# Storing the second half of the last nine output tiles from ScalarE's queue

## The chip, the core and the metric

The kernel runs on one core of a Trainium2 chip. The core has five engines with instruction streams of their own: TensorE (PE in the profile), VectorE (DVE), ScalarE (ACT), GpSimd (POOL) and SyncE (SP). They meet only at semaphores. SyncE computes nothing; here it issues DMAs. Sixteen DMA engines move the data of all queues. The metric is the device time of one execution in microseconds (us); lower is better.

## What is computed

```python
scores = scale * np.matmul(q_c, k_c.transpose(0, 1, 2, 4, 3))   # chunks of 64 positions
attn = softmax(scores)
x = (attn @ v_c), heads side by side                            # [8, 576, 512]
theta = x @ w_theta
zr, zi = x * np.cos(theta), x * np.sin(theta)
y = einsum('ts,bsd->btd', w_tok_r, zr) + einsum('ts,bsd->btd', w_tok_i, zi)
u = x + y
out = u + np.maximum(u @ w_ch, 0.0)                             # [8, 576, 512] float32
```

The inputs `q`, `k`, `v` have the shape 8 x 8 x 576 x 64 in float32. The first three lines are attention within chunks of 64 positions; the rest mixes positions (`w_tok_r`, `w_tok_i`) and channels (`w_theta`, `w_ch`).

## The kernel before

The eight batches are worked in four pairs, `p` = 0 to 3 (`NP` is 4). A pair has 1152 positions, cut into nine tiles of 128 rows, numbered `j` = 0 to 8. Tile 4 (`MID`) is shared by both batches; every other tile belongs to one batch and holds two blocks of 64 positions that lie 128 positions apart in the output. So a result tile has two row halves, `half[0]` (partitions 0 to 63) and `half[1]` (64 to 127), and each half goes to another place of the output.

The order of all work is written out by hand in the list `ORDER`. A step such as `W.35.0` names the work, the pair, the tile and, where needed, a buffer slot; the instructions of each engine follow this list. The last part of the list works on pair 3 and holds, for each tile, these steps:

- `Y` (line 482): 9 accumulating matmuls of 512 columns (18 of half the rows for tile 4) give y on TensorE.
- `y` (line 490): VectorE adds x and writes the tile `u`.
- `Ud` (line 507): SyncE issues a DMA transpose of `u` into `uT`. For the last tile, 30, TensorE transposes instead (`U`, line 499), and VectorE copies (`uv`, line 513).
- `W` (line 519): 4 matmuls with `w_ch`.
- `w` (line 528): VectorE computes max(., 0) + u and writes the float32 tile `o32`, of which there are four buffers.
- `st` (line 543): two DMAs, one for each row half, store the tile.
- `D` (line 156): a matmul on a blank tile, whose result nothing uses.

SyncE's queue holds, in the order of the list, the stores of line 543 and the DMA transposes of lines 400 and 507. The list ends as follows (the last line holds the end of the program):

```text
Ud.35 W.35.0 Ud.37 st.38 W.36.1 w.35 st.35 w.36 st.36 W.37.0 U.30.1 uv.30 w.37 W.30.1
D.00.0 D.00.0 D.00.0 D.00.0 st.37 w.30 st.30 D.00.1 D.00.0 D.00.1 D.00.0 D.00.1 D.00.0
```

Each DMA has a completion semaphore, one of a small set that is used in turn. At the end of the program SyncE waits for all landings, and then the engines meet at a barrier (both appear under line 623). ScalarE issues no DMA in this kernel: it computes exponentials, sines and cosines, and some copies. Its last compute instruction is the sine of step `g.3D`, which stands in the list ahead of the first store of pair 3 (`st.32`).

Of the kernel before, what the change touches and what calls it, by code (L numbers as in the profile page):

```python
# [68 lines left out]
def kernel(  # L69
# [11 lines left out]
    nc = tc.nc  # L81
# [6 lines left out]
    NP = B // 2  # L88
# [18 lines left out]
    half = [slice(0, CH), slice(CH, P)]  # L107
# [425 lines left out]
    def store(p, j):  # L533
        o = st[p].pop(("o", j))
        if j == MID:
            to = [out[2 * p + b, KT * P : S, :] for b in range(2)]
        else:
            bb = int(j > MID)
            jl = j - bb * (MID + 1)
            s0 = (jl // 2) * GT + (jl % 2) * CH  # L540
            to = [out[2 * p + bb, s0 + r * P : s0 + r * P + CH, :] for r in range(2)]
        for r in range(2):
            nc.sync.dma_start(to[r], o[half[r]])  # L543

# [42 lines left out]
        "W": w,  # L589
        "w": relu_add,  # L590
        "st": store,
    }
    with tc.manual_schedule():
# [34 lines left out]
```

## Time and profile before

| What | us |
|---|---|
| median of 6 runs | 212.7 |
| lowest and highest of them | 211.34, 214.14 |
| the profiled execution | 213.83 |
| its span, first to last instruction | 212.1 |
| TensorE busy in it | 194.5 |
| VectorE busy | 134.4 |
| ScalarE busy | 89.1 |
| GpSimd busy | 105.4 |

The profiled execution is one run of its own; 1.7 us of its time lie outside the span. The engine names end in q where an instruction is the sequencer's own: it waits, or issues a DMA, and the engine is not counted as busy. A DMA's row gives when its issue begins and how long the queue is held; when the data have landed is told apart, as the time from the beginning of the issue. The 72 stores of line 543 have 128.0 KB each (64 rows of 2 KB), and land 2.5 us after their issue began, in the median.

### The profile page before, as it was taken

The numbers are of one execution on the slowest core, as the hardware profiler recorded it, in microseconds if no ns is written. First come the engines' busy times: TensorE is split into PE (matmuls) and PEld (weight loads), VectorE is DVE, ScalarE is ACT, GpSimd is POOL, SyncE is SP. The second block draws the span as 40 slices with busy tenths as digits, with TensorE's granted clock in tenths as the row PEclk, the third lists the DMA queues.
The fourth block names the chain that finished last, engine by engine and source line by source line (L and its number), as shares of the span: only waits on it lengthen the run. The fifth ranks groups of instructions, "written<-read, shape, count | busy, mean of one in ns | idle before, by whom it ended". The sixth has DMA issues, their size and how long they took to land.

```text
span 212.1 us, 6378 instructions
## 1 busy us (share of the span) xinstructions
PE 194.5 (92%) x2790; PEld 96.8 (46%) x2790; DVE 134.4 (63%) x243; ACT 89.1 (42%) x91; POOL 105.4 (50%) x131
## 2 busy tenths in 40 slices
PE   7838879999999999999999999949969999999983
PEld 2414435655555654455554555414434443444431
DVE  1402856978878948987773997545864762845360
ACT  2004477455923477857319929643002563000000
POOL 8799989988998999789799000000000000000000
PEclk9995899999999999999999999987999999999999
DMA  6999999999999999999999920684668677845756
GB/s 199 273 154 146 151 173 160 166 165 163 169 202 151 139 169 180 200 188 200 152 156 201 148 49 2 151 106 96 143 96 168 128 149 150 179 96 121 152 117 144
DMA packets 137947, 32.09 MB, mean 151 GB/s; under 512 B 130624, under 2 KB 132288, under 8 KB 137920
## 3 DMA queue, kind: packets, MB, share of 16 engines
q0 software_dynamic: 113744, 15.43, 114.0%
q1 hardware_dynamic: 24176, 16.26, 33.8%
q8 instruction: 22, 0.36, 0.7%
q14 instruction: 5, 0.04, 0.1%
HBM read 33.06 MB, written 9.44 MB: 200 GB/s over the span
## 4 chain that ended last, share of the span: by engine, by line
PE 67%; DMA 15%; POOL 8%; DVE 4%; issue 3%; SPq 2%; ACT 0%; POOLq 0%
PE ps_y L482 27%; PE ps_theta L413 12%; PE ps_uw L519 12%; DMA qk<-in_k_dram 7%; POOL qk L173 5%; PE ps_idle L156 4%; PE ps_qkT L269 4%; DMA qk<-in_q_dram 3%; DMA xT<-x 3%; POOL v L181 3%; PE ps_sT L315 3%; PE ps_x L348 3%; DMA uT<-u 2%; SPq L543 1%; PE ps_uT L499 1%
## 5 line engine op out<-in xcount | busy, mean ns | idle before, releaser
L482 PEld LDWEIGHTS <-wT 128*128 128x128 f16 (+1 forms) x360 | 30.8, 100 | 35.2 <-issue 1.6
L482 PE MATMUL ps_y<-zr,wT 128*128 128x512 f16 (+1 forms) x180 | 45.0, 380 | 0.2 <-ACT uT L513 0.2
L482 PE MATMUL ps_y<-zi,wT 128*128 128x512 f16 (+1 forms) x180 | 42.0, 379 | 0.0
L490 DVE TENSOR_TENSOR u<-ps_y,x 128x512 f16<-128x512 f32 x36 | 24.7, 689 | 27.2 <-PE ps_y L482 27.2
L519 PE MATMUL ps_uw<-wch,uT 128*128 128x512 f16 x144 | 36.8, 386 | 3.5 <-DMA uT<-u 3.0
L173 POOL DMA_DIRECT2D qk<-in_q_dram x40 | 34.6, 898 | 5.4 <-PE ps_qkT L269 1.4
L413 PE MATMUL ps_theta<-wtheta,xT 128*128 128x512 f16 x144 | 34.6, 385 | 2.1 <-DMA xT<-x 2.1
L173 POOL DMA_DIRECT2D qk<-in_k_dram x40 | 34.6, 892 | 3.8 <-DMA qk<-in_q_dram 1.8
L181 POOL DMA_DIRECT2D v<-in_v_dram x40 | 34.4, 896 | 1.2 <-DMA v<-in_v_dram 0.5
L429 ACT ACTIVATE cos<-ps_theta,pihalf 128x1024 f16<-128x1024 f32 (+1 forms) x20 | 20.6, 1029 | 34.3 <-PE ps_theta L413 33.4
L328 ACT ACTIVATE eT<-ps_sT 128x1024 f16<-128x1024 f32 (+1 forms) x20 | 18.6, 938 | 35.2 <-PE ps_sT L315 35.1
L528 DVE SCALAR_TENSOR_TENSOR o<-ps_uw,u 128x512 f32<-128x512 f32 x36 | 24.7, 688 | 11.9 <-PE ps_uw L519 11.3
L361 DVE TENSOR_TENSOR x<-ps_x,recip 128x512 f16<-128x512 f32 (+1 forms) x40 | 25.5, 638 | 1.4
L413 PEld LDWEIGHTS <-xT 128*128 128x128 f16 x144 | 13.8, 100 | 19.9 <-DMA xT<-x 3.1
L519 PEld LDWEIGHTS <-uT 128*128 128x128 f16 x144 | 13.0, 98 | 18.5 <-DMA uT<-u 3.3
L156 PE MATMUL ps_idle<-blank 128*128 128x512 f16 x60 | 19.8, 459 | 1.4 <-DVE pihalf L144 1.2
L433 ACT ACTIVATE sin<-ps_theta 128x1024 f16<-128x1024 f32 (+1 forms) x20 | 18.7, 934 | 0.0
L294 DVE COPY qkT<-ps_qkT 128x2048 f16<-128x2048 f16 x12 | 14.6, 1220 | 5.6 <-PE ps_qkT L269 5.6
L269 PE MATMUL ps_qkT<-id,qk 64*128 64x64 f16 x576 | 12.4, 193 | 3.6 <-DMA qk<-in_k_dram 3.5
L269 PEld LDWEIGHTS <-qk 64*128 64x128 f16 x576 | 10.1, 96 | 7.9 <-DMA qk<-in_k_dram 3.9
L360 DVE RECIPROCAL recip<-ps_x 128x8 f32<-128x8 f32 (+1 forms) x40 | 7.8, 196 | 7.3 <-PE ps_x L348 7.1
L442 DVE TENSOR_TENSOR zr<-x,cos 128x1024 f16<-128x1024 f16 x16 | 10.9, 684 | 1.0 <-ACT cos L429 1.0
(43 smaller groups left out, 138.2 us busy)
## 6 DMA issues: line engine op xcount, KB each, us to landing
out_dram<-o SPq DMA_DIRECT2D x72, 128.0 KB, 2.5
qk<-in_q_dram POOLq DMA_DIRECT2D x32, 128.0 KB, 7.0
qk<-in_k_dram POOLq DMA_DIRECT2D x32, 128.0 KB, 6.4
v<-in_v_dram POOLq DMA_DIRECT2D x32, 128.0 KB, 6.1
theta<-in_moe_w_theta_dram SPq DMA_DIRECT2D x1, 1024.0 KB, 8.4
tok<-in_moe_w_tok_i_dram SPq DMA_DIRECT2D x1, 576.0 KB, 4.1
tok<-in_moe_w_tok_r_dram SPq DMA_DIRECT2D x1, 576.0 KB, 5.3
qk<-in_q_dram POOLq DMA_DIRECT2D x8, 64.0 KB, 8.6
```

The source lines that it names most:

```text
L156: nc.tensor.matmul(ps, blank[:, 0:P], blank, start=True, stop=True)
L173: nc.gpsimd.dma_start(nats[p, g][rows, which, r], (q, k)[which][b, :, t0 : t0 + n, :].rearrange("h s d -> s h d"),)
L181: nc.gpsimd.dma_start(v16[rows, slot + r, :, 0:D], v[b, :, t0 : t0 + n, :].rearrange("h s d -> s h d"),)
L269: nc.tensor.transpose(psv[:, r, w, e, j, :], t[half[r], w, j, 2 * e : 2 * e + 2, :].rearrange("s h d -> s (h d)"), id16[half[r], half[r]],)
L361: nc.vector.tensor_tensor(out=st[p]["x"][:, j0 : j0 + n, f * NE * D : (f + 1) * NE * D].rearrange("p c (h d) -> p c h d", h=NE), in0=psv[: ...
L413: nc.tensor.matmul(ps[:, j * DM : j * DM + DM], xT[:, j * NDB + db, :], wtheta16[:, db, :], start=(db == 0), stop=(db == NDB - 1),)
L429: nc.scalar.activation(out=cos[:, 0:n].rearrange("p a e -> p (a e)"), in_=pin, func=AF.Sin, bias=pihalf, scale=1.0,)
L433: nc.scalar.activation(out=sin[:, 0:n].rearrange("p a e -> p (a e)"), in_=pin, func=AF.Sin)
L482: nc.tensor.matmul(ps[rows], wT[:, kt, cols], z[:, jz, :], start=(kt == 0), stop=(kt == 2 * KT),)
L490: nc.vector.tensor_tensor(out=u, in0=st[p].pop(("ps_y", j))[:, 0:DM], in1=st[p]["x"][:, j], op=ALU.add)
L519: nc.tensor.matmul(ps, uT[:, db * P : db * P + P], wch16[:, db, :], start=(db == 0), stop=(db == NDB - 1),)
L528: nc.vector.scalar_tensor_tensor(out=o, in0=st[p].pop(("ps_uw", j)), scalar=0.0, in1=u, op0=ALU.max, op1=ALU.add)
```

## The change

In pair 3 (`p == NP - 1`), the store of the second row half (`r == 1`) of each of the nine tiles is issued from ScalarE's queue; the store of the first half stays in SyncE's. Nine of the 72 stores move. The addresses, the sizes and the list `ORDER` stay as they are.

```diff
         for r in range(2):
-            nc.sync.dma_start(to[r], o[half[r]])
+            queue = nc.scalar if p == NP - 1 and r else nc.sync
+            queue.dma_start(to[r], o[half[r]])
```

## The prediction

> **What bounds the kernel now.** I read the chain of work that ended last first, because only what lies on it is worth time, and then its last stretch in order of time. By engine, the chain is this:
>
> ```profile
> PE 67%; DMA 15%; POOL 8%; DVE 4%; issue 3%; SPq 2%; ACT 0%; POOLq 0%
> ```
>
> Most of it is TensorE. The stores of pair 3 begin at 189.3 us, so only the end matters. The table of waits says whether TensorE waits for anything there (window 176.5 to 206 us; columns: who, for whom, us in total, times, longest):
>
> ```profile
> PE ps_uw L519 <- DVE uT L513: 0.5, 1, 0.5
> PE ps_theta L413 <- DMA xT<-x: 0.4, 1, 0.4
> ```
>
> The second wait is over before the first store of pair 3, and the first is the VectorE copy of tile 30. From 180 to 200 us TensorE is busy 5.00 of every 5.00 us. So no store and no transpose on SyncE holds TensorE, and a freer SyncE cannot make the matmuls earlier. What is left is the tail behind the last matmul. Three views show it: VectorE's timeline, SyncE's timeline, and the line of the final waits (start, duration, engine, line, what; in the last two rows min/median/max in ns, then first and last start).
>
> ```profile
> 204.98 0.68 DVE L528 SCALAR_TENSOR_TENSOR o<-ps_uw,u 128x512 f32<-128x512 f32 x1
> 206.20 0.69 DVE L528 SCALAR_TENSOR_TENSOR o<-ps_uw,u 128x512 f32<-128x512 f32 x1 [0.53 <-PE ps_uw L519]
> ```
>
> ```profile
> 203.25 0.47 SPq L543 DMA_DIRECT2D out_dram<-o  x1
> 203.77 1.59 SPq L543 DMA_DIRECT2D out_dram<-o  x1
> 205.46 0.55 SPq L543 DMA_DIRECT2D out_dram<-o  x1
> 206.74 2.47 SPq L543 DMA_DIRECT2D out_dram<-o  x4
> 208.62 0.59 SPq L543 DMA_DIRECT2D out_dram<-o  x1
> ```
>
> ```profile
> L623 SPq EVENT_SEMAPHORE  x12: 17/28/28, 209.3 to 212.0; - x12
> L623 PEldq DRAIN  x2: 13/222/430, 208.6 to 211.6; - x2
> ```
>
> The last result tile (30) is ready at 206.20 + 0.69 = 206.89. SyncE begins its two stores only at 208.03 and 208.62: it is 1.14 us late, because it still has the stores of 36 (ready 204.17, issued from 205.46) and 37 (ready 204.98 + 0.68 = 205.66, issued 206.74 and 207.34) in hand. Neighbouring stores start about 0.64 us apart, so a tile costs SyncE 1.28 us, and tiles 35, 36, 37 and 30 come 0.94, 1.49 and 1.23 us apart. On top, one issue took 1.59 us instead of 0.59. The trace's packets show a 16 KB instruction packet from 203.76 to 204.99; five other stores that began in such a packet (at 110.84, 120.12, 132.90, 153.34 and 177.97) took 1.05 to 1.72 us and ended some 0.4 us after it, as this one did.
>
> The last store lands at about 208.62 + 2.35 = 210.97 (its own landing is not recorded; second halves beside it land after 2.3 to 2.4 us, and SyncE's wait ends at 211.0). From there to the end of the span at 212.06 are 1.09 us of last waits and barrier.
>
> **The change, part by part.**
>
> *Removed from SyncE:* nine issues of 0.59 us, 5.3 us in all. Ahead of 201 us this only makes the transposes of 35 and 37 start earlier; TensorE does not wait for them, so the worth is nothing. If that cover were gone (a transpose landing later than its matmuls are due), the least margin is that of tile 35: landing 198.53 + 2.4 = 200.9, used at 201.5, 0.5 us. The change takes issues out from ahead of it, so the margin grows.
>
> *Added to ScalarE:* nine issues. ScalarE's last compute instruction starts at 179.47 and takes 1.02 us; the first moved store is ready after 189 us. Each new store waits for VectorE's result, and behind that wait stand only later stores and the final barrier. Nobody else waits for ScalarE. Its cost is nothing until the last tile.
>
> *Semaphores:* completion semaphores are reused every eighth DMA, and each issue waits for the one before on its semaphore. The closest case is the very last store: its predecessor on the semaphore was issued at 201.77 and landed at about 204.1, 2.8 us before 206.9. No stall. A second set of semaphores would give SyncE up to eight more final waits of some 0.06 us (their spacing); those ahead of the last landing are hidden, so 0 to 0.3 us, taken as nothing.
>
> *The tail, with both queues issuing at once.* Tile 35: both halves at 203.25; SyncE's takes 0.47, so both can be through before the packet at 203.76. Tile 36: ready at 204.17, inside the packet, both held to about 205.37. Tile 37: ready at 205.66, both begin at 205.69 and end by 206.28. Tile 30: ready at 206.89, both queues are free and begin at 206.92 (SyncE follows VectorE by 0.03 us at 203.25). The 1.1 us of lateness is gone, and the second half no longer stands behind the first.
>
> Landing of tile 30: a store whose queue was waiting for it lands 2.24 us after its start (that of 192.74), so the first at 209.16. The second half's data move beside it. At the 273 GB/s of the page's busiest slice 128 KB need 0.48 us, so both have landed by 209.16 + 0.48 = 209.64. If the halves overlap wholly, it is 209.16. I take 209.6, because the two share the DMA engines. Gain: 210.97 - 209.6 = 1.4 us; bounds 1.3 and 1.8. TensorE's last blank matmul and its drain end at 208.6 + 0.43 = 209.0, so they don't take over as the end.
>
> *ScalarE's issue time* is the unknown: the trace has no DMA issued there. From below, SyncE's own 0.47 us; from above, the longest ordinary issue of another kind, 1.24 us for a DMA transpose. With 1.24 us its stores of 35 to 30 begin at 203.25, about 204.5 (held to 205.8 at most), 205.8 and 207.0, and the last lands some 0.7 us after a short one: gain 0.7. I take SyncE's value, as the instruction is the same, and keep 0.7 for the range.
>
> *Two rules that speak against the change.* The row: SyncE's 0.59 us is held per store, whatever it moves, since the 1 MB load of w_theta took less:
>
> ```profile
> 1.75 0.47 SPq L212 DMA_DIRECT2D theta<-in_moe_w_theta_dram  x1
> ```
>
> The Trainium skill, "DMA: Bandwidth & Descriptors", section "Rules for kernel authors", says of two transfers to disjoint partition halves: "Don't bother — they serialize", and that several issuing engines only save issue time. By that rule the data gain nothing (I have let them serialize: 0.48 us), and all that counts is issue time. Here issue time is what is late, so the sum stays 1.4. The sharper rule is in "Perfetto Trace Analysis", section "DMA Instruction — HWDGE (DVE, Sync)": one descriptor generator is shared by the two issuing sequencers and locked while one uses it. If the lock covers the whole 0.59 us, ScalarE's second half of 35 runs into the instruction packet as now, and the six stores behind it follow one another from 205.37: 36 to 206.55, 37 to 207.73, and 30 begins its halves at 207.73 and 208.32 instead of 208.03 and 208.62. That is a gain of 0.3 us. Against it stands the row above: eight times the rows of a store (512 of 2 KB against 64) in no more time, so that making descriptors is a small part of an issue and the lock short. I go by the row: 1.4, not 0.3. No run here shows two issuing queues of this kind side by side.
>
> **The sum.** 213.83 - 1.4 = 212.4 us for the profiled execution, span 212.1 - 1.4 = 210.7. That execution lies 1.1 us above the median of the runs; the tail behind the last matmul does not depend on what made it longer, so the median goes from 212.7 to 211.3, 0.65% less.
>
> **The rivals.**
>
> *A, the shared generator serializes the issues.* Gain 0.3 us (0.1 to 0.7), median 212.4. For it: the rule. Against it: the 0.47 us for 1 MB.
>
> *B, slower: ScalarE issues slowly.* Place: its last four stores, from 203.25. They follow one another, so at T each the last begins at 203.25 + 3T. This passes today's 208.62 from T = 1.8 us on, three times SyncE's cost. At T = 2.4 the last begins at 210.45, 1.8 us later than now: 214.5. For it: GpSimd's issues take 0.89 us, so issues are not alike on all engines. Against it: no undisturbed issue in the trace takes over 1.24 us.
>
> *C, the forecast's gain with another beside it, over 1%.* The tail alone can give at most 206.92 + 2.24 = 209.16 against 210.97, 1.8 us or 0.85%. Over 1% would need something ahead of the tail, where I find no wait: 210.2. That the change does not do what it says (the moved stores not the last ones) is excluded by the list: `st.30` is the last store, and its second half moves.
>
> **How the numbers follow.** Forecast 0.66, A 0.18, B 0.08, C 0.08. Within 1% (about what a measurement of this kernel can tell from no change) are the forecast and A: 0.84. The forecast's own range is 210.9 to 212.0. The range reaches over A to 212.9, and down to 209.9, since the six runs of before already spread from 211.34 to 214.14; B's upper part and the lower part of C stay out.
>
> **What would show it.** Right: SyncE's last store begins at about 206.9 us and ScalarE's within 0.1 us of it, with issues of about 0.6 us; the last landing comes at about 209.6; TensorE's busy time and its last matmul stay. Wrong: ScalarE's issues of 1.1 us or more, beginning with SyncE's (the lock, A); ScalarE's stores running late behind one another (B); TensorE's matmuls with `w_ch` waiting for `uT`; or the end set by something other than the last landing.

## The result, and the profile after

The changed kernel took 211.64 us (median of 29 runs, 209.57 to 215.93) against 212.72 us (66 runs, 209.35 to 216.23) for the kernel before. The ratio is taken over the runs that lie within 1.5% of the fastest run of the same kernel, 31 of the 66 and 19 of the 29. It is 0.9974, with a 95% interval from 0.995 to 0.9999: a gain of 0.55 us, between 0.02 and 1.06. The forecast was 1.4 us. So the direction held, and the gain stayed within 1% as forecast, but its size was missed.

In the profile after, the execution took 210.01 us and its span 208.2 us. The page shows the second queue (queue, kind, packets, MB, share of 16 engines), and its chain of work that ended last, by engine:

```profile
q1 hardware_dynamic: 23456, 15.08, 30.6%
q10 hardware_dynamic: 720, 1.18, 2.2%
...
PE 80%; DMA 8%; DVE 4%; POOL 3%; issue 2%; SPq 2%; ACT 1%; ACTq 0%; POOLq 0%
```

TensorE carries the chain as before. Its table of waits in the last stage (174 to 203.5 us) is word for word that of before, so nothing was won or lost there:

```profile
PE ps_uw L519 <- DVE uT L513: 0.5, 1, 0.5
PE ps_theta L413 <- DMA xT<-x: 0.4, 1, 0.4
```

The tail, in the timelines of VectorE, SyncE and ScalarE (start, us, engine, line, what), for the last two results and the last two tiles' stores:

```profile
202.43 0.68 DVE L528 SCALAR_TENSOR_TENSOR o<-ps_uw,u 128x512 f32<-128x512 f32 x1
203.65 0.69 DVE L528 SCALAR_TENSOR_TENSOR o<-ps_uw,u 128x512 f32<-128x512 f32 x1 [0.54 <-PE ps_uw L519]
```

```profile
201.65 0.88 SPq L544 DMA_DIRECT2D out_dram<-o  x1
203.14 0.47 SPq L544 DMA_DIRECT2D out_dram<-o  x1
204.37 0.47 SPq L544 DMA_DIRECT2D out_dram<-o  x1
```

```profile
201.65 0.85 ACTq L544 DMA_DIRECT2D out_dram<-o  x1
203.15 0.50 ACTq L544 DMA_DIRECT2D out_dram<-o  x1
204.38 0.50 ACTq L544 DMA_DIRECT2D out_dram<-o  x1
```

The last result is ready at 203.65 + 0.69 = 204.34, and both queues begin its stores at once, 0.03 us later. Each issue is short, though the two run side by side. The line of the last pair of stores gives their landings (min/median/max of the two), and the line of the final waits gives the end:

```profile
DMA to landing us min/median/max: 2.4/2.5/2.7
```

```profile
L624 SPq EVENT_SEMAPHORE  x12: 17/28/28, 204.9 to 208.2; - x12
```

The halves land 2.39 and 2.70 us after their issue, the second at 207.08. That is 2.74 us after the last result; in before it was 210.97 - 206.89 = 4.08, by the prediction's estimate of the last landing.

Since executions differ ahead of the tail, I cut each span at two points: the first theta matmul of group 3D, which stands ahead of every instruction that the change touches, and the end of the last `w`.

| us | to the cut | middle | tail | span |
|---|---|---|---|---|
| before | 176.53 | 30.36 | 5.17 | 212.1 |
| after | 173.98 | 30.36 | 3.88 | 208.2 |

The middle, in which the nine moved stores are issued, is equal to 0.01 us. The tail is 1.29 us shorter. The other 2.55 us of the two spans' difference lie ahead of the change and are none of its doing. Outside the span the two executions need 1.77 and 1.79 us, so the change costs nothing there either.

### The profile page after: what moved, and what is told of

Same layout as the page of the kernel before. It is cut to its first block, busy times and chain, and to the rows that moved or that the text cites. A ratio compares the mean times of both kernels' runs of the same rounds, so it can differ in the third digit from the quotient of the medians.

```text
span 208.2 us, 6386 instructions
## 1 busy us (share of the span) xinstructions
PE 192.9 (93%) x2790; PEld 96.4 (46%) x2790; DVE 134.4 (65%) x243; ACT 89.1 (43%) x91; POOL 105.2 (51%) x131
## 4 chain that ended last, share of the span: by engine, by line
PE 80%; DMA 8%; DVE 4%; POOL 3%; issue 2%; SPq 2%; ACT 1%; ACTq 0%; POOLq 0%
PE ps_y L482 31%; PE ps_theta L413 15%; PE ps_uw L519 14%; PE ps_qkT L269 5%; PE ps_idle L156 4%; DMA qk<-in_k_dram 4%; PE ps_x L348 3%; PE ps_sT L315 3%; POOL qk L173 3%; DMA xT<-x 3%; DMA uT<-u 2%; PE ps_uT L499 2%; PE ps_xT L379 2%; DVE x L361 1%; SPq L544 1%
## 5 line engine op out<-in xcount | busy, mean ns | idle before, releaser
L519 PE MATMUL ps_uw<-wch,uT 128*128 128x512 f16 x144 | 35.9, 380 | 2.9 <-DMA uT<-u 2.4
L413 PE MATMUL ps_theta<-wtheta,xT 128*128 128x512 f16 x144 | 33.9, 379 | 1.1 <-DMA xT<-x 1.1
```

The source lines that it names most:

```text
L413: nc.tensor.matmul(ps[:, j * DM : j * DM + DM], xT[:, j * NDB + db, :], wtheta16[:, db, :], start=(db == 0), stop=(db == NDB - 1),)
L519: nc.tensor.matmul(ps, uT[:, db * P : db * P + P], wch16[:, db, :], start=(db == 0), stop=(db == NDB - 1),)
```

## The experiments

The theories: **1**, the tail gains 1.0 to 1.35 us in every execution, and the comparison of full kernels is too coarse for it; **2**, the tail gains so much, but the second queue costs 0.6 to 0.8 us elsewhere; **3**, the tail of before hangs on a 16 KB instruction packet, so its first profile showed more lateness than there always is.

**Both kernels again (e1, e2).** No edit but a comment.

> The kernel before, once more, against itself. All theories: ratio 1.000. Looked at: the stretch from the end of the last w (line 528) to the end of the span, 5.17 us in the profile of before. Theory 1 (the tail gains 1.3 us in every execution and nothing else changes; the comparison is too coarse for it) and theory 2 (the tail gains 1.3 us, and something ahead of it costs 0.8 us) say 5.1 to 5.2 us again. Theory 3 (the length of the tail of before hangs on where the 16 KB instruction packet falls, and the profiled execution had a long one) says a shorter tail, 4.2 to 4.9 us.

> The changed kernel once more. Theory 1: tail 3.85 us, the stretch from the first theta matmul of group 3D to the end of the last w 30.4 us as in both profiles, ratio 0.9935 (0.991 to 0.996). Theory 2: that stretch, or the one before it, is 0.8 us longer than in before, ratio 0.997. Theory 3: tail 3.85 us and ratio 0.996 to 0.998, because the tail of before is usually shorter than in its first profile.

Measured: e1 against before 0.9976 (0.9911 to 1.0042), so a kernel against itself is known to no better than 0.65%. e2: 0.9989 (0.993 to 1.0047). These ratios decide nothing. The cuts do: e1 has a middle of 30.37 and a tail of 4.91, e2 has 30.46 and 3.82. SyncE's timeline in e1 shows the issue that meets the packet, and the last two stores; VectorE's row is the last result:

```profile
200.72 1.32 SPq L543 DMA_DIRECT2D out_dram<-o  x1
...
204.70 0.55 SPq L543 DMA_DIRECT2D out_dram<-o  x1
205.29 0.59 SPq L543 DMA_DIRECT2D out_dram<-o  x1
```

```profile
203.15 0.69 DVE L528 SCALAR_TENSOR_TENSOR o<-ps_uw,u 128x512 f32<-128x512 f32 x1 [0.54 <-PE ps_uw L519]
```

Here the packet took 1.02 us and not 1.23, the issue was held 1.32 us and not 1.59, and SyncE was 204.70 - 203.84 = 0.86 us late, not 1.14. So the lateness moves with the packet, and the gain is 1.09 us between these two. No middle is 0.8 us longer, which speaks against theory 2.

**Without the packet in the tail (e3, e4).** The first 24 `D` steps are taken out of `ORDER` in before (e3) and in the changed kernel (e4), so that the packet, which comes after a fixed number of TensorE instructions, falls behind the end.

```diff
-ones.00 D.00.0 D.00.1 lw.01 cw.01 lw.00 D.00.0 q.0M D.00.1 D.00.0 D.00.1 D.00.0 D.00.1
-D.00.0 D.00.1 D.00.0 q.0B q.0A cw.00 k.0M D.00.1 D.00.0 D.00.1 D.00.0 D.00.1 D.00.0
+ones.00   lw.01 cw.01 lw.00  q.0M     
+   q.0B q.0A cw.00 k.0M      
...
```

> The kernel before without the first 24 blank matmuls (D) at the start: 48 TensorE instructions fewer, so that the last 16 KB instruction packet, which comes 41 instructions ahead of the end, is not fetched within the tail. The reading that this packet holds SyncE's issue for 1.0 us (theories 1 and 3): no issue over 0.65 us in the last 10 us, the last stores begin at 0.03 and 0.6 us after the last w, tail 4.1 us in place of 5.2. Were the packet harmless, the tail would stay at 5.1 to 5.2. The total may move either way by the loss of the blank matmuls at the start, so the tail is what counts.

> The changed kernel without the same 24 blank matmuls. Both queues are free when the last tile is ready, with the packet or without: tail 3.85 us as in the changed kernel. So without the packet the change is worth only 0.25 us of tail against the kernel before without the packet (theories 1 and 3), or still 1.3 us if the packet is harmless.

Measured: tail 4.21 in e3 and 3.81 in e4. In e3's SyncE timeline the second store of tile 35 is now an ordinary one, and the last two follow the last result (ready at 204.26 + 0.69 = 204.95) by 0.14 and 0.74:

```profile
201.84 0.59 SPq L543 DMA_DIRECT2D out_dram<-o  x1
...
205.09 0.55 SPq L543 DMA_DIRECT2D out_dram<-o  x1
205.69 0.59 SPq L543 DMA_DIRECT2D out_dram<-o  x1
```

So the packet made 0.7 to 0.96 us of the tail of before, and the change is worth 0.40 us without it (expected 0.25). The totals (0.9981 and 1.0051, with intervals of 0.55 to 0.85% to each side) hold the loss of the blank matmuls too and say nothing.

**Pair 3 alone (e5, e6).** `ORDER` keeps the weights' steps, the blank matmuls and the steps of pair 3.

```diff
...
-D.00.1 lt.00 init.00 D.00.0 D.00.1 D.00.0 TW.00.0 twd.00 TW.01.1 D.00.1 D.00.0 D.00.1
-D.00.0 D.00.1 k.0B v.0M D.00.0 k.0A T.0M.2 tq.0M S.0M.0 D.00.1 twd.01 D.00.0 D.00.1 v.0B
+D.00.0 cw.00 D.00.1 D.00.0 D.00.1 D.00.0 D.00.1 D.00.0 D.00.1 lt.00 init.00 D.00.0 D.00.1 D.00.0
+TW.00.0 twd.00 TW.01.1 D.00.1 D.00.0 D.00.1 D.00.0 D.00.1 D.00.0 D.00.1 twd.01 D.00.0 D.00.1 D.00.0
...
```

> The kernel before with the work of pair 3 and the weights alone (pairs 0 to 2 are left out, two of eight batches are computed); its end is the same, instruction for instruction, and the last 16 KB packet falls at the same place. Far fewer loads stand ahead, so that its time should vary less. Both theories: tail from the end of the last w to the end of the span 4.9 to 5.2 us. Its time is to be set beside that of e6.

> The changed kernel with the work of pair 3 and the weights alone (pairs 0 to 2 left out). Tail 3.85 us. Theory 1 (the tail's gain reaches the whole time): its time is 1.0 to 1.35 us below that of e5. Theory 2 (a second queue costs some 0.6 to 0.8 us elsewhere, ahead of the tail or outside the span): 0.2 to 0.6 us below.

Measured: 102.21 us (101.39 to 103.63) and 100.90 us (99.67 to 101.19): 1.31 us apart in the median, 1.7 in the mean, with 6 runs each. Tails 5.24 and 3.96; middles 30.36 and 30.37. The whole time moves by about what the tail gained, as theory 1 says. The close agreement of 1.31 is in part luck: in the two profiles the first cuts come at 66.20 and 64.91 us, so as much again differs ahead of the change.

**Both halves from ScalarE (e9).** Against the changed kernel the edit is this:

```diff
-            queue = nc.scalar if p == NP - 1 and r else nc.sync
+            queue = nc.scalar if p == NP - 1 else nc.sync
```

> Both halves of pair 3's stores from ScalarE's queue; SyncE keeps only the transposes there. Theory that the gain comes from two queues issuing side by side: ScalarE is now the late queue, tail 4.9 to 5.2 us as before. Theory that it comes from taking the stores out from behind SyncE's transposes: tail 3.9 to 4.2 us.

Measured: tail 4.93, middle 30.36. ScalarE's timeline shows the same backlog as SyncE's before: the packet holds its issue, and the last stores begin 0.87 us and 1.46 us after the last result (206.81 + 0.69 = 207.50).

```profile
204.39 1.28 ACTq L544 DMA_DIRECT2D out_dram<-o  x1
...
208.37 0.55 ACTq L544 DMA_DIRECT2D out_dram<-o  x1
208.96 0.61 ACTq L544 DMA_DIRECT2D out_dram<-o  x1
```

So the gain is that two queues issue side by side. Taking the stores out from behind SyncE's transposes brings nothing.

**A smaller last tile (e8).** To see whether more is to be had, tile 30's `W`, `w` and `st` work in two column halves.

```diff
+            for c in range(2):
+                for r in range(2):
+                    (nc.sync, nc.scalar)[r].dma_start(
+                        to[r][:, c * 256 : c * 256 + 256], o[c][half[r]]
+                    )
```

> The changed kernel, with the last tile (30) worked in two column halves of 256: two groups of 4 matmuls, two w, four stores of 64 KB (first row half from SyncE, second from ScalarE). The first column half is ready 0.4 us earlier, the last w is half as long, and the last stores are half as large. From the start of the last copy of line 513 to the end of the span: 7.4 us in before, 6.1 in the changed kernel, expected here 5.6 (5.5 to 5.8), if the landing after the last issue is 2.2 to 2.4 us for half the bytes; 6.1 or more if each further issue costs what it saves.

Measured: 6.10 us from the copy to the end, where the changed kernel has 6.13 and 6.06; ratio to before 1.0006 (0.9969 to 1.0044). It missed. The last two rows of VectorE's and of ScalarE's timelines show why:

```profile
205.83 0.42 DVE L547 SCALAR_TENSOR_TENSOR o32c<-ps_uw,u 128x256 f32<-128x256 f32 x1
206.41 0.42 DVE L547 SCALAR_TENSOR_TENSOR o<-ps_uw,u 128x256 f32<-128x256 f32 x1 [0.15 <-PE ps_uw L522]
```

```profile
206.35 0.78 ACTq L571 DMA_DIRECT2D out_dram<-o32c  x1
207.22 0.58 ACTq L571 DMA_DIRECT2D out_dram<-o  x1
```

The last result is ready at 206.83, 0.12 us earlier relative to the copy (2.13 us after its start, and 2.25 in the changed kernel), but ScalarE is still busy with the first column half and begins the second at 207.22. A store of 64 KB then lands 2.47 us later, where the last one of 128 KB took 2.70 us in after and 2.62 in e2. The further issue costs about what the smaller piece saves.

**The end alone (e10 to e13).** To be rid of the loads, pair 3's steps from `Y` on run on constants. Ahead of them stand 227 `D` steps (e10, e11) or 200 (e12, e13).

```diff
+    def constants(p):
+        for name in ("x", "zr", "zi"):
+            nc.vector.memset(st[p][name], 0.25)
+        nc.vector.memset(wT, 0.25)
+        nc.vector.memset(wch16, 0.25)
```

> Only the end of the kernel before: the steps Y, y, Ud, U, uv, W, w, st of pair 3 and the blank matmuls between them, on constants that VectorE writes; all loads, the attention, theta and pairs 0 to 2 are left out, and 227 blank matmuls stand ahead, so that the last 16 KB packet comes as far from the end as in before. No load is left that could vary. Tail from the end of the last w to the end of the span 4.9 to 5.2 us. Its time is the base for e11.

> The same end (loads, attention, theta and pairs 0 to 2 left out) with the second row halves stored from ScalarE. Theory 1 (the tail's gain reaches the whole time): 1.0 to 1.35 us below e10, tail 3.8 to 3.9 us. Theory 2 (the second queue costs 0.6 to 0.8 us outside the tail): 0.2 to 0.6 us below.

> e10 with 27 blank matmuls fewer at the start (54 TensorE instructions), so that the program ends before a further 16 KB packet is fetched in the tail; the same parts are left out. Tail 4.2 us. Its time is the base for the next kernel.

> e11 with the same 27 blank matmuls fewer (the same parts left out). Tail 3.8 us; its time 0.4 us below that of e12 (0.3 to 0.5). So two thirds of what the change brings would hang on the packet. Were the packet of no weight, the difference would be the 1.0 to 1.35 us of e10 and e11.

Measured, medians of 5 runs: 87.84 and 86.73 us with the packet (1.11 apart, tails 4.91 and 3.62), 81.69 and 80.52 without (1.17 apart, tails 4.06 and 3.61). The first pair agrees with its tails. The second does not: the tail shows 0.45, the time 1.17. The runs of one kernel still lie 0.75 to 1.3 us apart, so one end is too small to be measured like this. That left the packet's share of the whole time open.

**Three ends in a row (e14 to e17).** The end of e10 to e13 three times, each begun by the last landing of the one before. The first line of `link` writes into the buffer of tile 30, so it waits for both its stores:

```diff
+    def link(p):
+        nc.vector.memset(st[p]["last"], 0.0)
+        nc.vector.tensor_copy(out=blank, in_=st[p]["last"])
```

> The end of e10 (constants, pair 3's steps from Y on; loads, attention, theta and pairs 0 to 2 left out) three times in a row. Between two ends VectorE writes into the buffer of the last stored tile, which waits for both its stores to land, and copies it into the tile that the next blank matmuls read, so that TensorE starts the next end only after the last landing. The blank matmuls in between place a 16 KB packet in each end as in before. Base for e15; about 250 us.

> The same three ends (the same parts left out), second row halves from ScalarE. Theory 1 (each last landing comes 1.0 to 1.35 us earlier and the whole time follows): 3.0 to 4.0 us below e14. Theory 2 as a single cost of 0.65 us for the program: 2.4 to 3.4 us; the comparison of the full kernels taken literally, 0.55 us a landing: 1.6 us.

> e14 with 27 blank matmuls fewer at the very start (the same parts left out), so that the 16 KB packets come 54 TensorE instructions later relative to each end, out of the last 6 us of each. Base for e17.

> e15 with the 27 blank matmuls fewer (the same parts left out). If the packet makes two thirds of the gain (0.40 to 0.45 us a landing without it): 1.2 to 1.4 us below e16. If the packet carries no weight in the whole time, as e12 against e13 could be read: 3.0 to 4.0 us, as in e15.

Measured: 207.65 against 202.28 us (5.37 apart), and without the packet 200.32 against 196.74 (3.58 apart). Both are more than any theory said. The traces split the two spans' differences:

| us | e14 - e15 | e16 - e17 |
|---|---|---|
| from the last `w` to the link or the end, three times | 3.35 | 1.41 |
| from link to next `Y`, twice | 1.69 | 1.82 |
| from start to first `Y` | 0.63 | 0.90 |
| span | 5.68 | 4.15 |

The first row is the change: 1.12 us a landing with the packet, 0.47 without, as theory 1 and theory 3 say. From each first `Y` to the last `w` all four need 28.62 to 28.64 us, so the second queue costs nothing there, and theory 2 is out. The third row lies ahead of the change and is scatter: in e10 to e13 the first `Y` came 0.11 and 0.58 us later with the change. The second row lies almost wholly in one gap of blank matmuls in each of e14 and e16. The windows around that gap of e14 (from:to, length, busy us of PE, PEld, DVE, POOL with counts, then the granted TensorE clock, DMA share, GB/s) show what happens:

```profile
142.00:145.30 3.30, 0.12 (x1) 0.00 (x0) 0.91 (x2) 0.00 (x0) 1.00 0.39 90
145.30:148.70 3.40, 3.35 (x9) 1.30 (x10) 0.00 (x0) 0.00 (x0) 0.54 0.00 0
148.70:152.10 3.40, 3.40 (x17) 1.44 (x16) 0.00 (x0) 0.00 (x0) 0.96 0.00 0
```

TensorE stood idle for 3.23 us, waiting for the late landing, and then ran some 3.4 us at half clock, which cost 1.7 us. In e15 the wait is 1.92 us there, and the granted clock stays at 1.00. The mean clock of the single runs agrees: it is 0.983 to 0.992 in all twelve of e14 and e16, and 1.00 in all twelve of e15 and e17. So the earlier landing also spared a clock drop, which belongs to my chain of three ends and not to the kernel, which ends with its last landing.

**Where the full comparison blurs.** The same drop stands in the full kernel, ahead of the change. In the first profile of before, TensorE waits at 139 to 142 us, and the next window has half the clock (these rows have ScalarE's busy time too, before GpSimd's):

```profile
139.00:142.00 3.00, 0.38 (x40) 0.26 (x26) 1.41 (x4) 1.28 (x1) 0.00 (x0) 1.00 0.92 76
142.00:145.00 3.00, 2.61 (x7) 0.97 (x8) 0.69 (x2) 0.00 (x0) 0.00 (x0) 0.50 0.59 117
```

From 120 to 160 us the mean granted clock is 0.96 in before and in e2, and 1.00 in after and in e1; their first cuts come at 176.53, 177.34, 173.98 and 173.47 us. So the drop falls on either kernel. By the rule of the Trainium skill ("TensorE: Matmul & The Clock Gate", Part 1), TensorE goes to half rate after an idle window of some 3.4 us. The runs show drops after shorter waits, and not after each: after 3.23 us in e14 and 2.32 us in e16, none after 3.02 us in e14's first gap or 2.51 us in e16's second, and none after the waits of e15 and e17, which are about 2 us at most. The measurement decides: here a wait of 2.3 us can do it.

Which waits do it depends on where they fall. Where an execution has two drops, their starts lie a whole multiple of 3.413 us apart: 126.29 us, or 37 steps, in before and in e2, and 40.96 us, or 12 steps, in e4. I cut each execution into such steps, counted from its drops. These are the steps that hold the wait ahead of the change, first in before, then in after:

```profile
138.56:141.97 3.41, 0.82 (x42) 0.47 (x40) 1.64 (x5) 1.70 (x2) 0.00 (x0) 1.00 0.95 93
```

```profile
137.97:141.38 3.41, 1.97 (x47) 0.96 (x45) 2.80 (x7) 2.70 (x3) 0.00 (x0) 1.00 0.94 153
141.38:144.79 3.41, 2.49 (x12) 1.19 (x13) 1.40 (x3) 0.00 (x0) 0.00 (x0) 1.00 0.43 79
```

In before the wait of 3.01 us lies in one step, in which TensorE is busy for only 0.82 us, and the next step runs at half clock. It is the same in e2 (0.59 us busy). In after the wait of 2.35 us is split between two steps, as is that of 2.55 us in e1 (2.15 and 2.12 us busy), and no drop follows. Length alone does not decide it: in e8 a wait of 2.62 us, hardly longer than e1's, lies in one step (0.79 us busy) and has its drop. e14 and e16 fit: 0.21 and 1.09 us busy in the step ahead of the drop, 1.40 and at least 2.05 in the steps of the waits without one. Near 1.4 us busy it went either way (a drop after 1.38 us in e9). So a like wait costs 1.7 us or nothing by where it falls on these steps, and they lie differently in each execution, whichever the kernel. This is read from the traces afterwards; no run was made to test it.

Each drop takes about 0.8% off the mean granted clock of a run, so the full kernels' runs can be sorted by the number of drops. With one drop (clock 0.990 to 0.992) the averages of before and of the changed kernel are 0.64 us apart, with two (0.982 to 0.984) 0.73, with three (0.976) 1.23, all in favour of the change. The middle group, 25 and 21 runs, is known to 0.7 us either way.

## Why the prediction was wrong in its size

Right, step by step: the chain ends in SyncE's backlog; TensorE is not touched (middle 30.36 in both); both last stores begin 0.03 us after the last `w` (0.03 and 0.035 measured); the last landing 2.75 us after it (2.74); 0.48 us for the second half's data (2.70 - 2.24 = 0.46, but 2.62 - 2.24 = 0.38 in e2, so this closeness is luck); 1.09 us from landing to end (1.14).

Rival A, the shared generator that serializes the issues, is out: issues that began 4 to 5 ns apart took 0.47 and 0.50 us, against 0.47 for one alone. The row of the 1 MB load was the better guide than the rule. Rival B is out as well: ScalarE's issues outside a packet take 0.47 to 0.78 us (the longest in e8), far from 1.8. C did not come about. Two readings were slightly off and change nothing: the longest issue outside a packet is a transpose of 1.39 us, at 136.65, and not of 1.24, and the stores that began in a packet include two more, at 92.62 and 93.14, which took only 0.47 and 0.65 us.

**The steps that failed** are two. The first is "SyncE [...] is 1.14 us late" as the base of "Gain: 210.97 - 209.6 = 1.4 us; bounds 1.3 and 1.8". I saw the instruction packet within that lateness, and still took the lateness of one execution as a constant. In the programs that end as the full kernel does (before, e1, e5, e10, packets of 1.02 to 1.23 us) SyncE is 0.86 to 1.14 us late and the tail is 4.91 to 5.24 us long; with the change it is 3.62 to 3.96. The four pairs differ by 1.09 to 1.29, on average 1.24. Without the packet 0.40 to 0.47 is left. So about two thirds of the gain is relief from a delay that falls there because of the number of instructions ahead of it, in every execution of this program and not in one of another length. This step explains only 0.16 us of the miss.

The second step is "the tail behind the last matmul does not depend on what made it longer, so the median goes from 212.7 to 211.3". It carries the tail's gain into the comparison of whole runs without any allowance, though the six runs it had spread over 2.8 us. The comparison gave 0.55 us, and from 1.24 to 0.55 no trace shows a place where time is lost: the middle is equal, and so is the time outside the span. What stands ahead of the cut scatters by more than that, with a drop of 1.7 us in some executions and not in others.

The interval of 0.02 to 1.06 us is also too narrow, because which runs enter the ratio hangs on the one fastest run of each kernel. Over all runs the medians are 1.08 us apart and the means 0.59. An estimate from the recorded times: I draw both kernels' runs from the 66 of before, take 1.24 us off those that stand for the changed kernel, and form the difference in the same way. It lies between 0.1 and 2.1 us in 95% of the draws, and at 0.55 or less in one of six. So 0.55 us does not speak against 1.24, nor does it show it.

In the programs with less ahead of the tail the time follows the tail in two pairs (1.31 and 1.11 us) and not in e12 and e13 (1.17 us, where the tails differ by 0.45); in the three ends the split of the spans shows it (1.12 a landing). That scatter alone makes the gap in the full kernel is argued and not shown, and what the change is worth there stays open between about 0.5 and 1.2 us.

## What to carry to other kernels

When an engine's queue issues the last stores, compare when the last result is ready with when its last store begins: what lies between is all that a second queue can win, and it is won only if the two queues can issue at the same time. Before taking that lateness from one profile, look for an issue that is longer than its neighbours and ask whether it will be there, and as long, in the next execution. Here, a gain of half a per cent was better measured by cutting the spans at points that the change cannot touch than by comparing whole times, because the clock drops ahead of the cut moved the time by more than that.

## What the runs showed of the hardware

The issue of a store that begins while a 16 KB instruction packet is under way mostly ends about 0.4 us after the packet, whichever queue issues it: it took 1.59 us on SyncE in before, 0.88 and 0.85 us on SyncE and ScalarE at once in after, 1.28 us on ScalarE in e9. Two queues did not escape it; they only had nothing in hand afterwards. Of 65 such stores in all traces, 58 ended 0.3 to 0.6 us after their packet; the other seven took their ordinary 0.47 us, and what sets them apart stays open.

Halving the last store from 128 to 64 KB, with other stores in flight both times, brought its landing forward by only 0.15 to 0.23 us (from 2.62 and 2.70 to 2.47).
